# Moving elementwise work of a chunked linear attention from GpSimd to VectorE and ScalarE, and four more chunks from float16 parts

## The chip, the cores and the metric

The kernel runs on one core of one Trainium2 chip. The time is the device time of one execution in microseconds; the runs of the kernel before have a median of 1040.34 us (1038.24 to 1041.38, three runs). The engines are written as in the profile: PE is TensorE (PEld its weight loads), DVE is VectorE, ACT is ScalarE, POOL is GpSimd, SP is SyncE, which issues most of the DMAs.

## What is computed

Three layers follow one another, for 4 batches, 768 tokens and 384 features (8 heads of 48). The first is a linear attention whose state is multiplied by a complex decay at every token; the second and third are MLPs with a hidden size of 1536, each behind a mixing of the tokens.

```python
mag = sqrt(a_re**2 + a_im**2); scale = minimum(mag, 0.999) / (mag + 1e-6)
for t in range(S):                       # S = 768, state D x D = 48 x 48 per head
    S_re, S_im = ar*S_re - ai*S_im + outer(k[t], v[t]), ar*S_im + ai*S_re
    y[t] = q[t] @ S_re
x = y as (batch, token, 384)
u = x + (x^T @ U @ V)^T                  # low rank: U is 768 x 32, V is 32 x 768
x1 = u + relu(u @ w1) @ w2               # first MoE
u = x1 + real(fft2(x1)); un = normalised rows of u
out = u + relu(un @ w1') @ w2'           # second MoE
```

## The kernel before

**Attention.** The tokens of a batch are cut into 6 chunks of 128, and elementwise work is done for a pair of chunks at a time, on tiles of 128 partitions by 3 x 2 x 128 = 768 columns. Pairs are numbered m = 0 to 11; pairs 0 to 2 are batch 0. `decays(m)` takes logarithms and exponentials of the decays, scans their running product along the tokens (L340) and makes decayed queries and keys; `turns(m)` makes the angles, scans their running sum (L381), takes sine and cosine and writes the turned queries and keys as `QK`, one tile a chunk (L408, L409). Six DMAs a chunk, issued on SP, rearrange `QK` to `QT`, heads apart. `products(m, j)` then does one chunk: scores, masked scores, keys turned back by PE, output and next state. A chunk is "plain" where its products are plain float32; otherwise each operand is split into a float16 part and a float16 remainder, and three float16 products replace one. Before, the chunks of batch 0 and the first four of batch 1 are plain: `plain = b == 0 or b == 1 and c < 4`.

**MoE.** `moe_units` goes over batches, two halves of 384 tokens (g) and 12 blocks of hidden units (f). In a hidden step PE makes `hp` (nine matmuls), ACT its rectified high part `hh` (L182), DVE the low part `hl` (L184), and PE adds the step before to `acc` (nine matmuls of `hh`, `hl` and weights). High and low parts are float32 values cut to what PE multiplies exactly; L91, L92 and L93 are the three products of such pairs. `make_ut` makes the input of a half: transposed tokens plus the low-rank mixing, as high and low parts. `from_f64` unpacks weights that lie in DRAM as float64 words.

**Order.** The first MoE's loop for batch b weaves in the attention of batch b+1 at a fixed rate (`Side`, 58 or 48 steps over 40 slots), so that both share every engine; in batch 3's half g = 1 it weaves in the second MoE's weights and the DFT of batch 0. Each engine's instructions are put in an order before the run, by a planner that goes by priorities and its own costs; on the chip each engine takes its queue in that order, so an instruction that waits holds up all behind it. `hh` and `hl` are traced with high priority. Which engine takes an elementwise step is written out in place, as in

```python
E = G if b else V                                  # decays: L325 on POOL from pair 3 on
(G if m == 2 or b else V).tensor_tensor(th, s1_, th, ALU.mult)          # L349
(G if m in (1, 2) or b else V).tensor_tensor(s1_, s1_, s2_, ALU.mult)   # L354
(V if z else G).tensor_tensor(QK[:, z, :, 128:256], ...)                # L409
G.tensor_tensor(plo[:, hs], pm[hf], ph[:, hs], ALU.subtract)            # L446
```

The functions that the change touches stand here with the profile's line numbers; each float32 tile with the tag "t" takes one of six buffers that all pairs share.

Of the kernel before, what the change touches and what calls it, by code (L numbers as in the profile page):

```python
# [8 lines left out]
F16 = mybir.dt.float16  # L9
# [4 lines left out]
I16 = mybir.dt.int16  # L14
AF = mybir.ActivationFunctionType
# [6 lines left out]
DM = H * D  # L22
# [19 lines left out]
def mixer_kernel(ctx, tc, a_in, qk_in, v_in, u_in, v4_in, w_in, cc_in, ss_in, cb_in, sb_in, id_in, mask_in, rows_in, out):  # L42
# [69 lines left out]
    def from_f64(src, name, signs=False):  # L112
# [22 lines left out]
    def load_w(mi, f, z):  # L135
# [4 lines left out]
        x = from_f64(w_in[mi, f][:, zs], f"w{mi}_{f}_{z}", mi == 1 or f > 8)  # L140
# [50 lines left out]
    # ------------------------------------------------------------------ attention  # L191
# [27 lines left out]
    def load(kind, m):  # L219
        """Decays, or queries and keys, of a pair of chunks."""  # L220
# [11 lines left out]
    def load_vs():  # L232
        """All values of the first batch."""
# [18 lines left out]

    def parts(m):
        """The first pair goes chunk by chunk, so that its products start early."""
        return [slice(0, 1), slice(1, 2)] if m == 0 else [slice(0, 2)]

    def decays(m):
        """Decayed queries and keys of a pair of chunks and the tangents of its turns."""
# [3 lines left out]
        E = G if b else V  # L262

# [3 lines left out]
        if b == 0:  # L267
            T_, s1, s2 = a[:, 1], mk("L"), mk("s")
# [4 lines left out]
        Th = a[:, 0] if b == 0 else mk("Th")  # L273
# [3 lines left out]
        ew[m] = T_, Th, qf, kf, ends  # L277
# [947 lines left out]
```

## Time and profile before

| | |
|---|---|
| median of the runs | 1040.34 us |
| span of the profiled execution, first to last instruction | 1035.1 us (5.2 us under the median of the runs) |
| mean granted clock of TensorE | 0.949 |
| busy, share of the span | PE 86%, PEld 81%, DVE 67%, ACT 43%, POOL 43% |
| instructions | DVE 1104, ACT 841, POOL 426, PE 6338 |
| first hidden step of the first MoE | about 137.8 us |
| first hidden step of the second MoE | about 694.6 us |

Busy shares are means over stages with different limits. Where a share matters below, it is read for one stage. An engine's time is not lost by idling; what is lost is read from what ended the idle time. A span on POOL is rough, and the matmuls' ends are modelled.

### The profile page before, as it was taken

The numbers are of one execution on the slowest core, as the hardware profiler recorded it, in microseconds if no ns is written. First come the engines' busy times: TensorE is split into PE (matmuls) and PEld (weight loads), VectorE is DVE, ScalarE is ACT, GpSimd is POOL, SyncE is SP. The second block draws the span as 40 slices with busy tenths as digits, with TensorE's granted clock in tenths as the row PEclk, the third lists the DMA queues.
The fourth block names the chain that finished last, engine by engine and source line by source line (L and its number), as shares of the span: only waits on it lengthen the run. The fifth ranks groups of instructions, "written<-read, shape, count | busy, mean of one in ns | idle before, by whom it ended". The sixth has DMA issues, their size and how long they took to land. (4 is left out here: it accounts for less than half of the span.)

```text
span 1035.1 us, 16471 instructions
## 1 busy us (share of the span) xinstructions
PE 885.1 (86%) x6338; PEld 841.7 (81%) x6338; DVE 690.3 (67%) x1104; ACT 441.3 (43%) x841; POOL 443.3 (43%) x426
## 2 busy tenths in 40 slices
PE   0059978788778787798899999779999999999997
PEld 0048777578777787787899999779999999999997
DVE  7997988897877689788764727886535554362121
ACT  6436565657545555555643224465212211222111
POOL 4445646575464645656446307776312222020000
PEclk9999899979898898989899999889999999999999
DMA  8078646834516152614135103342101021000000
GB/s 346 0 103 165 194 81 138 166 69 109 94 45 121 49 93 69 115 48 93 33 61 200 39 1 115 108 144 77 62 16 47 2 77 46 1 23 19 7 23 27
DMA packets 47097, 83.43 MB, mean 81 GB/s; under 512 B 5600, under 2 KB 36064, under 8 KB 47008
## 3 DMA queue, kind: packets, MB, share of 16 engines
q1 hardware_dynamic: 45152, 75.96, 30.8%
q0 software_dynamic: 1856, 6.31, 1.7%
q8 instruction: 52, 0.85, 0.4%
q14 instruction: 37, 0.30, 0.1%
HBM read 53.79 MB, written 9.44 MB: 61 GB/s over the span
## 5 line engine op out<-in xcount | busy, mean ns | idle before, releaser
L184 DVE SCALAR_TENSOR_TENSOR hl<-hp,hh 128x384 fp32r<-128x384 f32 x192 | 105.4, 551 | 191.8 <-ACT hh L182 186.6
L182 ACT ACTIVATE hh<-hp 128x384 fp32r<-128x384 f32 x192 | 93.1, 488 | 270.9 <-PE hp L93 249.1
L91 PE MATMUL acc<-w,hh 128*128 128x384 f32 x576 | 202.4, 352 | 2.0 <-ACT hh L182 2.0
L93 PE MATMUL acc<-w,hl 128*128 128x384 f32 x576 | 166.1, 352 | 38.4 <-DVE hl L184 38.2
L92 PE MATMUL acc<-w,hh 128*128 128x384 f32 x576 | 197.4, 343 | 0.0
L93 PEld LDWEIGHTS acc<-w,hl 128*128 128x128 f32 x576 | 106.9, 195 | 45.4 <-DVE hl L184 45.1
L91 PEld LDWEIGHTS acc<-w,hh 128*128 128x128 f32 x576 | 111.4, 193 | 4.3 <-ACT hh L182 3.0
L92 PEld LDWEIGHTS acc<-w,hh 128*128 128x128 f32 x576 | 111.5, 194 | 0.0
L91 PE MATMUL hp<-u,w 128*128 128x384 f32 x288 | 103.0, 359 | 6.2 <-ACT w L141 3.1
L92 PE MATMUL hp<-u,w 128*128 128x384 f32 x288 | 103.7, 360 | 1.2 <-POOL u L630 1.0
L93 PE MATMUL hp<-u,w 128*128 128x384 f32 x288 | 102.4, 356 | 0.0
L92 PE MATMUL hp<-n,w 128*128 128x384 f32 x288 | 96.9, 336 | 1.6 <-DVE n L920 1.6
L91 PE MATMUL hp<-n,w 128*128 128x384 f32 x288 | 96.5, 336 | 1.1 <-ACT n L919 1.1
L93 PE MATMUL hp<-n,w 128*128 128x384 f32 x288 | 96.8, 336 | 0.0
L437 PE MATMUL sc<-QT 96*128 96x128 f32 x384 | 66.6, 328 | 11.4 <-DMA QT<-QK 10.5
L437 PEld LDWEIGHTS sc<-QT 96*128 96x128 f32 x384 | 60.7, 232 | 14.3 <-issue 11.3
L142 POOL TENSOR_TENSOR w<-wxw,w 128x384 fp32r<-128x384 f32 x48 | 58.8, 1235 | 21.9 <-ACT w L141 21.7
L451 PE MATMUL kp<-ident,QK 128*128 128x128 f32 x120 | 20.5, 297 | 53.7 <-POOL QK L409 48.6
L91 PEld LDWEIGHTS hp<-u,w 128*128 128x128 f32 x288 | 58.5, 203 | 7.0 <-ACT w L141 3.3
L451 PEld LDWEIGHTS kp<-ident,QK 128*128 128x128 f32 x120 | 16.1, 155 | 55.5 <-POOL QK L409 48.6
L92 PEld LDWEIGHTS hp<-u,w 128*128 128x128 f32 x288 | 58.6, 203 | 2.2 <-POOL u L630 1.6
L93 PEld LDWEIGHTS hp<-u,w 128*128 128x128 f32 x288 | 58.3, 203 | 0.0
(302 smaller groups left out, 2056.4 us busy)
## 6 DMA issues: line engine op xcount, KB each, us to landing
QT<-QK SPq DMA_DIRECT2D x144, 129.0 KB
stw<-in_w_dram SPq DMA_DIRECT2D x48, 384.0 KB
ain<-in_a_dram SPq DMA_DIRECT2D x12, 768.0 KB
qkin<-in_qk_dram SPq DMA_DIRECT2D x12, 768.0 KB
x1d<-x SPq DMA_DIRECT2D x24, 192.0 KB
vin<-in_v_dram SPq DMA_DIRECT2D x18, 192.0 KB
lo<-x1d SPq DMA_DIRECT2D x12, 192.0 KB
out_dram<-lo SPq DMA_DIRECT2D x12, 192.0 KB
```

The costliest lines, as they stand in the source:

```text
L91: T.matmul(o, ah, bh, start=start, stop=False, skip_group_check=skip)
L92: T.matmul(o, ah, bl, start=False, stop=False, skip_group_check=skip)
L93: T.matmul(o, al, bh, start=False, stop=stop, skip_group_check=skip)
L142: G.tensor_tensor(w[:, 1, zs], x, f32(w[:, 0, zs]), ALU.subtract)
L182: A.activation(hh, hp, AF.Relu)
L184: V.scalar_tensor_tensor(out=hl, in0=hp, scalar=0.0, in1=f32(hh), op0=ALU.max, op1=ALU.subtract)
L437: T.matmul(ps[:, h, :], q[:, 128:256], q[:, :128], start=True, stop=True)
L451: T.transpose(kp[z][:, i * 128 : (i + 1) * 128], QK[:, z, i, 128:256], ident)
```

## The change

Work moves between engines, and four chunks change their arithmetic. From pair 3 on, POOL keeps the tangent (L337) and the decayed key (L360) of a pair, the small `fe` of a chunk and the weights' low parts; DVE takes the products L349 and L354, both halves of the turned keys, the remainders `plo`, `S[2]` and `slo`, the scaling of the state (except in batch 0) and the low part of u. ACT takes the multiply-add of L325, the rounding multiply of L389, the two range checks in place of L291, and the in-place scaling of the keys in `QK` (L494) as three passes of a [P, 1] scale. The three scans of a pair become one over 768 columns, with uint8 multipliers that restart each row; queries and keys are turned by sine and cosine in one instruction of 768 columns each, for which both lie in one tile `turn`. The tag "t" goes from six buffers to four and `turn` takes the room of the other two. In `make_ut` the low-rank product is added in PSUM, on top of the transposes, so that the copy of `xs` and the addition on DVE go. Weights are given their sign by a bit operation on DVE, always. All of batch 1's chunks are made from float16 parts.

```diff
-        if signs:
-            A.activation(high.bitcast(F32), high.bitcast(F32), AF.Sign)
-            G.tensor_tensor(x, x, high.bitcast(F32), ALU.mult)
-        else:
-            V.scalar_tensor_tensor(out=xi, in0=high, scalar=-(2**31), in1=xi, op0=ALU.bitwise_and, op1=ALU.bitwise_or)
+        V.scalar_tensor_tensor(out=xi, in0=high, scalar=-(2**31), in1=xi, op0=ALU.bitwise_and, op1=ALU.bitwise_or)
...
-        def at(nm, tag=None, bufs=6, shape=(128, 3, 2, 128), dt=F32, pl=pl):
+        def at(nm, tag=None, bufs=4, shape=(128, 3, 2, 128), dt=F32, pl=pl):
...
-            T_, s1, s2 = mk("T"), mk("L"), mk("s")
+            turn = at(f"turn{b}_{cc[0]}", "turn", 1, (128, 2, 3, 2, 128))
+            T_, s1, s2 = turn[:, 1], mk("L"), mk("s")
...
-                steady(js)
+                if b == 0:
+                    steady(js)
+                else:
+                    A.activation(Th[:, :, js], re, AF.Relu, bias=least, scale=-1.0, accum_out=stat("im", b, cc[0]))
+                    A.activation(Th[:, :, js], s2_, AF.Relu, bias=most, accum_out=stat("im", b, cc[1]))
...
-            E.tensor_scalar(s2_, s2_, -2e-6, 1.0, ALU.mult, ALU.add)
+            A.activation(s2_, s2_, AF.Copy, bias=1.0, scale=-2e-6)
...
-            for i in range(3):
-                V.tensor_tensor_scan(out=row(s1, i, js), data0=starts[:, :n], data1=row(s1, i, js), initial=1.0, op0=ALU.max, op1=ALU.mult)
+            V.tensor_tensor_scan(out=flat(s1), data0=starts, data1=flat(s1), initial=1.0, op0=ALU.max, op1=ALU.mult)
...
-            (G if m == 2 or b else V).tensor_tensor(th, s1_, th, ALU.mult)
+            V.scalar_tensor_tensor(out=th, in0=s1_, scalar=FSCALE**2, in1=th, op0=ALU.mult, op1=ALU.mult)
...
-            (G if m in (1, 2) or b else V).tensor_tensor(s1_, s1_, s2_, ALU.mult)
+            V.scalar_tensor_tensor(out=s1_, in0=s1_, scalar=FSCALE**2, in1=s2_, op0=ALU.mult, op1=ALU.mult)
...
-            (G if m in (1, 2, 3, 4) else V).tensor_tensor(f, q, s1_, ALU.mult)
+            (G if m in (1, 2) else V).tensor_tensor(f, q, s1_, ALU.mult)
...
+            if len(jj) == 1:
+                if cy is not None:
+                    V.tensor_tensor(T_[:, :, 0, 0], T_[:, :, 0, 0], cy[:, :3], ALU.add)
+                V.tensor_tensor_scan(out=flat(Th), data0=going, data1=flat(T_), initial=0.0, op0=ALU.mult, op1=ALU.add)
...
-            V.tensor_scalar(t, th, 1.0 / (2 * PI), MAGIC, ALU.mult, ALU.add)
+            if b == 0:
+                V.tensor_scalar(t, th, 1.0 / (2 * PI), MAGIC, ALU.mult, ALU.add)
+            else:
+                A.activation(t, th, AF.Copy, bias=MAGIC, scale=1.0 / (2 * PI))
...
-                for z, w in ((1, T_), (0, Th)):
-                    V.tensor_tensor(QK[:, z, :, :128], qf[:, :, j], w[:, :, j], ALU.mult)
-                    (V if z else G).tensor_tensor(QK[:, z, :, 128:256], kf[:, :, j], w[:, :, j], ALU.mult)
+                w = turn[:, :, :, j]
+                for to, x in ((slice(128, 256), kf), (slice(0, 128), qf)):
+                    V.tensor_tensor(QK[:, :, :, to], x[:, :, j].unsqueeze(1).to_broadcast([128, 2, 3, 128]), w, ALU.mult)
+                for z in range(2):
                     for i in range(3):
                         p0 = z * 48 + i * 16
                         nc.sync.dma_start(QT[p0 : p0 + 16], QK[:, z, i, :])
...
-        plain = b == 0 or b == 1 and c < 4
+        plain = b == 0
...
-                G.tensor_tensor(plo[:, hs], pm[hf], ph[:, hs], ALU.subtract)
+                V.tensor_tensor(plo[:, hs], pm[hf], ph[:, hs], ALU.subtract)
...
-                for z in range(2):
-                    G.tensor_tensor(QK[:, z, :, 128:256], QK[:, z, :, 128:256], QK[:, z, :, 256:257].to_broadcast([128, 3, 128]), ALU.mult)
+                for i in range(3):
+                    A.activation(QK[:, :, i, 128:256], QK[:, :, i, 128:256], AF.Copy, scale=QK[:, 0, i, 256:257])
...
-                    G.tensor_tensor(sh, pS.rearrange("p (h e) -> p h e", h=8), f3, ALU.mult)
+                    V.tensor_tensor(sh, pS.rearrange("p (h e) -> p h e", h=8), f3, ALU.mult)
...
-            G.tensor_tensor(slo, sS, shi, ALU.subtract)
+            V.tensor_tensor(slo, sS, shi, ALU.subtract)
...
         def mix(k):
-            zv = bank(f"zv{b}_{g}_{k}")[:, :384]
-            T.matmul(zv, zst[b][:, k * 128 : (k + 1) * 128], vst[:, g * 384 : (g + 1) * 384], start=True, stop=True)
-            V.tensor_tensor(xs[k], zv, xs[k], ALU.add)
+            zv = bank(f"zv{b}_{g}_{k}")[:, :384] if first else xs[k]
+            T.matmul(
+                zv,
+                zst[b][:, k * 128 : (k + 1) * 128],
+                vst[:, g * 384 : (g + 1) * 384],
+                start=first,
+                stop=True,
+                skip_group_check=not first,
+            )
+            if first:
+                V.tensor_tensor(xs[k], zv, xs[k], ALU.add)
             u = pair(f"u{b}_{g}_{k}")
             A.copy(u[:, 0], xs[k])
-            (V if (b, g) == (0, 0) else G).tensor_tensor(u[:, 1], xs[k], f32(u[:, 0]), ALU.subtract)
+            V.tensor_tensor(u[:, 1], xs[k], f32(u[:, 0]), ALU.subtract)
```

Here `first` is true for batch 0's first half alone. `turn` of batch 0 is the tile of the decays, except for pair 2. The filling matmuls that run while PE has nothing to do keep their number and size, with other operands.

## Rows read from the trace of the kernel before

**Rows 1.** Stretches: us, busy time (instructions) of each engine, PE's granted clock, DMA.
```profile
0.00:137.80 137.80, 72.67 (x702) 59.32 (x703) 119.71 (x172) 73.28 (x131) 68.57 (x59) 0.96 0.59 152
137.80:315.80 178.00, 144.53 (x1134) 131.94 (x1132) 151.19 (x200) 104.79 (x188) 104.75 (x81) 0.90 0.51 107
315.80:463.80 148.00, 123.48 (x990) 116.89 (x989) 115.95 (x150) 83.21 (x152) 82.33 (x73) 0.89 0.38 75
463.80:583.80 120.00, 110.56 (x922) 107.39 (x922) 84.67 (x125) 57.06 (x112) 67.44 (x73) 0.96 0.38 92
...
627.70:694.60 66.90, 56.04 (x304) 52.85 (x304) 60.83 (x111) 32.28 (x69) 50.74 (x54) 0.91 0.39 121
```

**Rows 2.** Waits, total us, times, longest: 315.8 to 463.8, last row 137.8 to 315.8.
```profile
PE acc L93 <- DVE hl L184: 13.9, 6, 5.2
ACT s L87 <- DVE L L340: 13.4, 3, 7.6
DVE L L326 <- POOL s L325: 9.9, 2, 7.2
...
DVE L L326 <- POOL s L325: 6.3, 2, 5.4
```

**Rows 3.** Timeline of DVE and POOL (start, us, engine, line), around 36 and 131 us.
```profile
36.00 5.79 DVE L381 TENSOR_TENSOR_SCAN ain<-one,ain 128x128 f32<-128x128 f32 x3
37.72 1.91 POOL L360 TENSOR_TENSOR qkin<-qkin,s 128x768 f32<-128x768 f32 x1
...
44.39 0.94 DVE L313 SCALAR_TENSOR_TENSOR L<-s,L 128x768 f32<-128x768 f32 x1
...
45.67 1.22 DVE L381 TENSOR_TENSOR_SCAN ain<-one,cy,ain 128x128 f32<-128x128 f32 x3
...
131.82 1.49 DVE L627 TENSOR_TENSOR xs<-zv,xs 128x384 f32<-128x384 f32 x3 [0.53 <-PE zv L626]
...
136.04 1.85 DVE L381 TENSOR_TENSOR_SCAN Th<-one,T 128x256 f32<-128x256 f32 x3 [1.06 <-ACT T L87]
```

**Rows 4.** DVE's groups by form, whole run: busy us, mean ns, idle before.
```profile
L340 DVE TENSOR_TENSOR_SCAN L<-starts,L 128x256 f32<-128x256 bf16 x36 | 37.6, 1097 | 0.1
...
L381 DVE TENSOR_TENSOR_SCAN Th<-one,cy,T 128x256 f32<-128x256 f32 x18 | 29.5, 1683 | 0.0
...
L326 DVE SCALAR_TENSOR_TENSOR L<-L,s 128x768 f32<-128x768 f32 x12 | 26.3, 2189 | 17.0 <-POOL s L325 16.8
```

**Rows 5.** POOL's groups by form, 315.8 to 463.8 us.
```profile
L446 POOL TENSOR_TENSOR ph<-pm,ph 128x512 f16<-128x512 f32 x12 | 16.0, 1337 | 5.3 <-ACT ph L445 5.3
...
L409 POOL TENSOR_TENSOR QK<-s,Th 128x384 f32<-128x384 f32 x6 | 7.9, 1331 | 4.7 <-issue 2.7 <-ACT Th L87 2.0
L354 POOL TENSOR_TENSOR L<-L,s 128x768 f32<-128x768 f32 x3 | 7.9, 2648 | 1.8 <-DVE s L353 1.8
L630 POOL TENSOR_TENSOR u<-xs,u 128x384 fp32r<-128x384 f32 x6 | 7.6, 1270 | 4.4 <-ACT u L629 4.4
L568 POOL TENSOR_TENSOR Sl<-S,Sh 96x384 f16<-96x384 f32 x5 | 6.8, 1354 | 1.9 <-ACT Sh L567 1.9
L349 POOL TENSOR_TENSOR Th<-L,Th 128x768 f32<-128x768 f32 x3 | 5.5, 1828 | 10.2 <-ACT Th L348 10.2
```

**Rows 6.** ACT's groups by form, whole run: a pass of 768 columns.
```profile
L311 ACT ACTIVATE L<-ain 128x768 f32<-128x768 f32 x11 | 9.2, 833 | 3.9 <-DMA ain<-in_a_dram 3.9
```

**Rows 7.** Timeline of PE: state products of a plain and of a float16 chunk.
```profile
96.86 3.62 PE L469 MATMUL g<-vin,ke 128*64 128x48 f32 x32
...
381.50 0.36 PE L469 MATMUL g<-vh,kl 128*128 128x48 f16 x8
```

**Rows 8.** POOL's groups by form, whole run.
```profile
L128 POOL TENSOR_TENSOR wxw<-wxw,stw 128x384 f32<-128x384 f32 x30 | 32.3, 1078 | 24.1 <-DVE wxw L125 8.3 <-issue 6.3 <-ACT stw L127 2.9
...
L494 POOL TENSOR_TENSOR QK<-QK 128x384 f32<-128x384 f32 x22 | 19.9, 907 | 17.4 <-DMA QT<-QK 10.1 <-DVE hl L184 3.9 <-DVE kl L461 3.4
...
L491 POOL TENSOR_SCALAR fe<-QT 96x8 f32<-96x8 f32 x20 | 7.3, 366 | 41.4 <-DMA QT<-QK 30.5 <-DVE S L548 7.2 <-DVE hl L184 2.4
```

More of the change, by code (lines that the diff above doesn't have):

```diff
@@ L14 @@
 I16 = mybir.dt.int16
+U8 = mybir.dt.uint8
 AF = mybir.ActivationFunctionType
@@ L110, in kept, with from_f64 @@
             fn(*args, **kw)
-    def from_f64(src, name, signs=False):
+    def from_f64(src, name):
         n = src.shape[-1]
@@ L276, in decays @@
         jj = [slice(0, 2)]
-        ew[m] = T_, Th, qf, kf, ends
+        ew[m] = T_, Th, qf, kf, ends, a if b == 0 else turn
         def of(js, *xs):
@@ L288, in steady @@
         def steady(js):
-            re, s2_, th = of(js, a[:, 0], s2, Th)
+            re, s2_ = of(js, a[:, 0], s2)
             V.scalar_tensor_tensor(
-                out=th if b else unread(js), in0=s2_, scalar=RE_LEAST, in1=re, op0=ALU.add, op1=ALU.is_le, accum_out=stat("re", b, cc[js.start])
+                out=unread(js), in0=s2_, scalar=RE_LEAST, in1=re, op0=ALU.add, op1=ALU.is_le, accum_out=stat("re", b, cc[js.start])
             )
@@ L368, in turns @@
         at = attention_pool()
-        T_, Th, qf, kf, ends = ew[m]
+        T_, Th, qf, kf, ends, turn = ew[m]
         use(TRIG)
@@ L378, in turns @@
             t, th = T_[:, :, js], Th[:, :, js]
-            n = 128 * (js.stop - js.start)
-            for i in range(3):
-                V.tensor_tensor_scan(
-                    out=row(Th, i, js),
-                    data0=one.to_broadcast([128, n]),
-                    data1=row(T_, i, js),
-                    initial=0.0 if cy is None else cy[:, i : i + 1],
-                    op0=ALU.mult,
-                    op1=ALU.add,
-                )
-            V.tensor_scalar(t, th, 1.0 / (2 * PI), MAGIC, ALU.mult, ALU.add)
+            if len(jj) == 1:
+                if cy is not None:
+                    V.tensor_tensor(T_[:, :, 0, 0], T_[:, :, 0, 0], cy[:, :3], ALU.add)
+                V.tensor_tensor_scan(out=flat(Th), data0=going, data1=flat(T_), initial=0.0, op0=ALU.mult, op1=ALU.add)
+            else:
+                for i in range(3):
+                    V.tensor_tensor_scan(
+                        out=row(Th, i, js),
+                        data0=one.to_broadcast([128, 128]),
+                        data1=row(T_, i, js),
+                        initial=0.0 if cy is None else cy[:, i : i + 1],
+                        op0=ALU.mult,
+                        op1=ALU.add,
+                    )
+            if b == 0:
+                V.tensor_scalar(t, th, 1.0 / (2 * PI), MAGIC, ALU.mult, ALU.add)
+            else:
+                A.activation(t, th, AF.Copy, bias=MAGIC, scale=1.0 / (2 * PI))
             V.scalar_tensor_tensor(out=th, in0=t.bitcast(I16)[:, :, :, 0::2], scalar=-2 * PI, in1=th, op0=ALU.mult, op1=ALU.add)
@@ L492, in products @@
             if not plain:
-                for z in range(2):
-                    G.tensor_tensor(QK[:, z, :, 128:256], QK[:, z, :, 128:256], QK[:, z, :, 256:257].to_broadcast([128, 3, 128]), ALU.mult)
+                for i in range(3):
+                    A.activation(QK[:, :, i, 128:256], QK[:, :, i, 128:256], AF.Copy, scale=QK[:, 0, i, 256:257])
         yield
@@ L641, in make_ut @@
             return
-        turn(0)
-        yield
-        turn(1)
-        mix(0)
-        yield
-        turn(2)
-        yield
-        mix(1)
-        yield
-        mix(2)
-        yield
+        for k in range(3):
+            turn(k)
+            mix(k)
+            yield
+            if k < 2:
+                yield
     def extra1(b, g, t, acc):
@@ L949, in mixer_kernel @@
     attp = [apool.enter_context(tc.tile_pool(name="att", bufs=2)), None]
+    starts = attp[0].tile([128, 6, 128], U8, tag="starts", name="starts", bufs=1)
+    going = attp[0].tile([128, 3, 256], U8, tag="going", name="going", bufs=1)
+    for x, every, rest_ in ((starts, 1, 0), (going, 0, 1)):
+        G.memset(x, rest_)
+        G.memset(x[:, :, 0:1], every)
+    starts = starts.rearrange("p x t -> p (x t)")
+    going = going.rearrange("p i t -> p (i t)")
     first = ExitStack()
@@ L966, in mixer_kernel @@
             with tc.issue_after(after):
-                T.matmul(warm, starts[:, :128], starts, start=True, stop=True, skip_group_check=True)
+                T.matmul(warm, mask, wide.bitcast(F16), start=True, stop=True, skip_group_check=True)
     first.close()
```

52 lines of the change are left out of this document (33 added, 19 removed).

## Prediction

> **What bounds the kernel now.** I read the table of stretches first, cut where the hidden steps of each batch of the first MoE begin [rows 1]. The reader is to see two regimes ahead of 694.6 us. Up to 137.8 us the first batch's attention runs and DVE is busy 119.7 us. From there to 583.8 us the first MoE works on batches 0, 1 and 2 with the next batch's attention woven in; these stages take 178, 148 and 120 us. PE stands still for 33, 25 and 9 us of them and is granted 0.90, 0.89 and 0.96 of its clock; DVE is busy 151, 116 and 85 us. From 627.7 to 694.6 us, where the second MoE's weights are unpacked, DVE is busy 60.8 of 66.9 us. After that nothing which this change touches is left but the last weight pieces. So what the change is worth is decided before 694.6 us, mostly in DVE's queue.
>
> The waits of batch 1's stage say why [rows 2]: PE waits 13.9 us for `hl`, a short DVE instruction stuck behind long ones. DVE itself waits 9.9 us for one POOL instruction, L325 (6.3 us in batch 0's stage). ACT waits 13.4 us for DVE's scans, with the hidden step's `hh` queued behind.
>
> Then I asked why DVE is long. On the timeline three scans of 128 columns take 5.79 us while POOL runs one product after another, and the same three take 1.22 us ten microseconds later, when POOL is idle [rows 3]. The groups confirm it [rows 4]: scans of 256 columns average 1097 and 1683 ns, where three back to back take 1.85 us, 617 each; L326 averages 2189 ns, where another instruction of 768 columns takes 0.94 us [rows 3]. (1097-617)x36 + (1683-617)x18 + (2189-940)x12 = 17 + 19 + 15 = 51 us of DVE are lost in these three groups alone.
>
> The Trainium skill, "SBUF — State Buffer", section "Who interferes with whom", says that VectorE and GpSimd share a port pair as an exclusive lock: a VectorE instruction with two SBUF inputs and a GpSimd instruction that reads SBUF keep each other out for a whole instruction. The trace agrees: the scans of 5.79 us stand beside POOL products of 1.9 us each [rows 3]. By that rule nearly all overlap is lost time, which would give the first rival below; the rule also speaks against the change, since what moves to DVE has two SBUF inputs itself and can be kept out by what stays on POOL.
>
> **The price of a POOL microsecond.** How much DVE time comes back for each microsecond taken from POOL? From below: the three groups alone, 51 us, over the 374 busy us that POOL has in the five stretches of the table, 0.14. From above: all the time in which the two can coincide, and DVE is busy 78% of batch 1's stage (116 of 148), so 0.78. Other groups with two SBUF inputs (L291, L313, L353, L408, L409, L125) are left out of the lower bound, so it is too low; the MoE's own DVE instructions read PSUM, so the upper one is too high. I take 0.35.
>
> **The change, part by part.**
>
> *Taken from POOL.* In batch 1's stage the groups that go are L446, L409, L354, L630, L568 and L349, 16.0 + 7.9 + 7.9 + 7.6 + 6.8 + 5.5 us [rows 5], and ten of L494 at 0.91, 9 us [rows 8]: 61 of POOL's 82.3 us [rows 1]. At 0.35 DVE gets 21 us back. The other stages go by the same means: a pair of chunks frees 1.83 + 2.65 + 2x1.33 = 7.1, a float16 chunk 2x1.34 + 2x0.91 + 1.35 = 5.8, three mixing steps 3.8 us. The first batch's attention has one L349, two L354, six L409 (k with the cosine) and pair 3's decays: 19 us, 7 back. Batch 0's stage has four pairs, some three float16 chunks, six mixing steps and six sign products L128 of 1.08 [rows 8]: 28 + 17 + 8 + 6 = 59, 21 back. Batch 2's stage has two pairs, about four chunks and three steps: 41, 14 back. 627.7 to 694.6 has some 18 sign products: 19, 7 back.
>
> *Added to DVE.* Neighbouring DVE instructions overlap a little: three of 384 columns take 1.49 us in a row [rows 3], so I count 0.48 for 384 columns, 0.6 for 512 and 0.87 for 768. A pair from pair 3 on: L349 and L354 come (+1.74), the count of re (-0.87) and the rounding multiply (L389, about -0.5) go to ACT. Twice three scans become two long ones: the trace shows no scan of 768, so it lies between 1.85 us (three of 256 at no gain) and 0.87 (any instruction of 768); nearest is the first, and from (617-407)/128 = 1.6 ns a column, the 128s being 1.22/3 = 407, it comes to 1.45, so -0.8 for both. The carry add costs 0.2, and six products of 384 become four of 768, 2.9 to 3.5. Net +0.4 a pair. A float16 chunk: L446 twice, L556 and L568: 1.2 + 0.96 = +2.1. Low halves of u trade an add for a subtraction: 0. A sign product becomes one pass: +0.48. The four chunks of batch 1 that turn float16 add `vl`, two `kl` and `ql` (0.48 + 0.96 + 1.1), 2.5 each.
> Sums: first batch +1, with the copies of L325 going to ACT. Batch 0's stage: four chunks at 4.6, less 2 for the first, which has no state, +16; chunks 4 and 5, +3; six signs +3; four pairs +2: +24. Batch 1: 6x2.1 + 1 = +14. Batch 2: +11. 627.7 to 694.6: 18x0.48 = +9.
>
> *Added to ACT.* A pair: two more passes of 768 columns at 0.83 [rows 6] with an accumulator's read each, say 2x1.0, and the passes of L325 and L389 at 0.83: +3.7 us. A chunk: the in-place rescale as three passes of 256 columns, each between 0.28 (a third of 0.83) and 0.83; nearer the first: +1.2. ACT is busy 104.8 of 178 and 83.2 of 148 us [rows 1]; with four pairs, five rescales and float16 copies of about 13 us it comes to 139 of 178, with three pairs and six rescales to 101 of 148. Beside DVE's and PE's work that is covered as long as ACT does not wait; where it does, see the second rival.
>
> *PE.* The state products of a plain chunk take 3.62 us; of a float16 chunk eight take 0.36 from start to end, so 24 take at most 1.1 [rows 7]. Four chunks give 10 us or more. That lies in batch 0's stage, where DVE is the longer (151 against 145), so I count none; without that cover it is worth these 10. In `make_ut` the mixing product is the same matmul, now into the transposes' bank: 0 on PE, and on ACT a copy less.
>
> *Waits.* L325 moves behind its Exp on ACT, so L326 no longer waits for POOL: 9.9 and 6.3 us go [rows 2]; what is late next is ACT's copy, under 1 us a pair, so I credit 9 and 6. On four pairs of batch 0's stage two POOL products of 1.83 and 2.65 also become DVE ones of 0.87 in the chain to the turns, 11 us of latency; most of it hides under the MoE, I count 3. The QT transfers are the same six per chunk on SP, issued after the second product instead of after each: half a microsecond, counted 0.
>
> **The sum.** First batch -7 + 1 = -6. Batch 0's stage -21 + 24 - 6 - 3 = -6. Batch 1's -21 + 14 - 9 = -16. Batch 2's -14 + 11 = -3, and PE, busy 110.6 of 120 us, allows little more. 627.7 to 694.6: -7 + 9 = +2. Together -29 against the profiled span of 1035.1 us: 1006. The median of the runs shown is 1040.34 us, 5.2 over that span; with these around it **1011 us**.
>
> **The rivals.** About 0.3%, 3 us, is what a measurement of this kernel can tell from no change.
>
> *More comes back.* At 0.6, and with `hl` and the scans no longer late, PE sets the pace. The relief rises by 0.25x(19 + 59 + 61 + 19) = 40 us, batch 2 being capped: 971, and to 960 if PE's 10 us count too. For it: 5.79 against 1.22 us, and the waits of 13.9 and 13.4 us that hang on DVE alone [rows 2, 3]. Against: the moved work has the form that is kept out, with L360, L337 and the weights' low halves still on POOL.
>
> *ACT waits for transfers (slower).* The in-place rescale of k may not start before the QT transfers have read it. On POOL these transfers were waited for by `fe` (L491), 30.5 us over 20 chunks, and by the rescale after it, 10.1 us over 22 instructions, two a chunk [rows 8]: 1.5 + 0.9 = 2.4 us a chunk, with nothing urgent behind. On ACT `hh` stands behind it, and PE behind `hh`. 15 chunks at 2.4 us are 36 us, against the 29 gained: 1047, and up to 1060 where PE's clock falls with it. It decides from 2 us a chunk. Against: `hh` is put ahead with high priority, so the rescale will mostly come late.
>
> *DVE is filled (slower or same).* At 0.17 the five sums are -2, +5, -5, +4 and +6: +8, 1048 us; at 0.2 the sides cancel, 1037 to 1043. For it: DVE is already busy 85 and 91% in batch 0's stage and from 627.7 to 694.6 [rows 1], where the change adds most.
>
> **Chances.** Forecast 0.46, more comes back 0.25, ACT waits 0.12, DVE filled 0.07, cancelled 0.10. Faster 0.71, same 0.10, slower 0.19. The range runs from the upper end of the gain rival's half to the lower half of the slower ones, 974 to 1046; the forecast's own, at 0.28 to 0.45, is 995 to 1025.
>
> **What the changed profile would show.** Right: POOL under 25 us in batch 1's stage and DVE near 109, the mean of the instruction at L326 near 1 us, the waits for `hl` halved, batch 1's stage near 132 us and batch 0's near 172. Wrong: an ACT wait for QT<-QK above 2 us a chunk; batch 0's stage no shorter, with DVE at 160 us or more; 627.7 to 694.6 longer by over 5 us; or batch 0's stage under 155 us, which would say that the float16 chunks' PE time, counted as nothing, was on the path.

## The result, and the profile after

The changed kernel takes 1029.38 us (median of 10 runs, 1020.90 to 1037.73) against 1040.14 (10 runs, 1036.85 to 1042.35): ratio 0.9887, 95% interval 0.9859 to 0.9914. It is 10.8 us faster; forecast were 29. Its profiled execution spans 1027.8 us. I cut it where the hidden steps of each batch begin, as in [rows 1]; "best" is both_halves, one of four kernels of the experiments that take 994 to 996 us; its profiled execution spans 992.3. The ten runs of the changed kernel spread over 16.8 us, those of the kernel before over 5.5; the changed kernel's two longest ran at a granted clock of 0.925, its two shortest at 0.945 and 0.947, and no run tells what decides it.

| stage | before | forecast | after | best |
|---|---|---|---|---|
| first batch's attention | 137.8 | 131.8 | 144.1 | 133.7 |
| batch 0's | 178.0 | 172 | 177.4 | 173.4 |
| batch 1's | 148.0 | 132 | 134.3 | 126.1 |
| batch 2's | 120.0 | 117 | 123.7 | 111.6 |
| batch 3's, g = 0 | 43.9 | 43.9 | 43.4 | 43.4 |
| batch 3's, g = 1 | 66.9 | 69 | 62.0 | 62.1 |
| from the second MoE on | 340.5 | 340.5 | 342.9 | 342.0 |

The stretches of the changed kernel, columns as in [rows 1]:

```profile
0.00:144.10 144.10, 71.39 (x702) 57.41 (x703) 114.36 (x159) 78.79 (x143) 52.85 (x51) 0.88 0.59 146
144.10:321.50 177.40, 133.63 (x1009) 121.88 (x1008) 136.68 (x202) 129.57 (x234) 38.33 (x36) 0.84 0.52 103
321.50:455.80 134.30, 116.10 (x979) 110.03 (x978) 100.77 (x151) 96.88 (x178) 19.86 (x21) 0.94 0.47 89
455.80:579.50 123.70, 113.03 (x970) 107.98 (x970) 87.86 (x148) 65.08 (x125) 30.15 (x36) 0.94 0.39 87
622.90:684.90 62.00, 54.51 (x309) 50.29 (x308) 59.38 (x124) 25.91 (x54) 34.68 (x38) 0.97 0.43 129
```

Against [rows 1], DVE's busy time fell in these five from 532 to 499 us and POOL's from 374 to 176, but batch 0's stage kept its length. There DVE is 14.5 us less busy and PE 10.9, and PE stands still for 43.8 us instead of 33.5, at 0.84 of its clock instead of 0.90. So neither DVE's nor PE's work holds that stage, and I looked at the waits. Five of the whole run that the change bears on (us in total, times, longest):

```profile
ACT QK L509 <- DMA QT<-QK: 33.1, 28, 3.0
DVE S L571 <- POOL fe L506: 24.7, 6, 5.3
PE sc L452 <- DMA QT<-QK: 23.1, 6, 8.0
PE acc L94 <- DVE hl L181: 17.5, 14, 2.7
DVE QK L419 <- DMA QT<-QK: 10.3, 3, 4.0
```

L509 is the in-place rescale of the keys (L494 before), L571 the scaling of the state (L556), L452 the scores (L437), L506 `fe` (L491), L419 the first write into a new `QK` (L405). Four of the five wait for QT transfers, directly or through `fe`. The fifth, `hl`, is what the change was reckoned by, and it did fall, from 38.2 us in the whole run before, and in batch 1's stage from 13.9 [rows 2] to 3.0. One moment of the timeline of the changed kernel shows three of them at once, behind SP's transfers, on ACT, PE and DVE:

```profile
210.20 7.68 SPq L427 DMA_DIRECT2D QT<-QK  x12
...
216.86 0.51 ACT L509 ACTIVATE QK<-QK 128x256 f32<-128x256 f32 x1 [2.53 <-DMA QT<-QK]
...
219.13 2.85 PE L452 MATMUL sc<-QT 96*128 96x128 f32 x16 [3.09 <-DMA QT<-QK]
...
219.41 0.56 DVE L571 TENSOR_TENSOR S<-S,fe 96x384 f32<-96x384 f32 x1 [3.42 <-POOL fe L506]
```

Both chunks of a pair are sent in one block of twelve transfers, 0.64 us each on SP, and three engines stand behind it.

DVE's groups that answer to [rows 4] (busy us, mean ns, idle before):

```profile
L347 DVE TENSOR_TENSOR_SCAN L<-starts,L 128x768 f32<-128x768 uint8 x11 | 21.6, 1966 | 0.2
L389 DVE TENSOR_TENSOR_SCAN turn<-going,turn 128x768 f32<-128x768 uint8 x9 | 17.4, 1932 | 0.2 <-ACT turn L88 0.2
L334 DVE SCALAR_TENSOR_TENSOR L<-L,s 128x768 f32<-128x768 f32 x11 | 13.7, 1244 | 7.3 <-ACT s L333 7.3
```

### The profile page after: what moved, and what is told of

It is laid out like the page before. It is cut to its first block, busy times and chain, and to the rows that moved or that the text cites. A ratio compares the mean times of both kernels' runs of the same rounds, so it can differ in the third digit from the quotient of the medians.

```text
span 1027.8 us, 16147 instructions
## 1 busy us (share of the span) xinstructions
PE 866.9 (84%) x6250; PEld 820.4 (80%) x6250; DVE 665.8 (65%) x1142; ACT 480.9 (47%) x910; POOL 234.0 (23%) x257
## 4 chain that ended last, share of the span: by engine, by line
PE 53%; DVE 23%; DMA 10%; ACT 5%; issue 4%; SPq 4%; POOL 1%; DVEq 0%; POOLq 0%; ACTq 0%
DMA QT<-QK 7%; PE acc L94 7%; PE hp L93 7%; PE hp L94 7%; PE acc L92 7%; PE hp L92 7%; PE acc L93 6%; SPq L427 3%; PE sc L452 3%; DMA stw<-in_w_dram 2%; PE g L484 2%; PE y L484 2%; DVE f L839 1%; DVE QK L423 1%; DVE wxw L126 1%
## 5 line engine op out<-in xcount | busy, mean ns | idle before, releaser
L92 PE MATMUL acc<-w,hh 128*128 128x384 f32 x576 | 200.3, 348 | 8.0 <-ACT hh L179 7.9
L93 PE MATMUL acc<-w,hh 128*128 128x384 f32 x576 | 194.3, 338 | 0.0
L94 PE MATMUL acc<-w,hl 128*128 128x384 f32 x576 | 160.8, 349 | 17.8 <-DVE hl L181 17.5
L92 PEld LDWEIGHTS acc<-w,hh 128*128 128x128 f32 x576 | 108.9, 189 | 13.2 <-ACT hh L179 11.5
L93 PEld LDWEIGHTS acc<-w,hh 128*128 128x128 f32 x576 | 109.0, 190 | 0.5 <-POOL w L139 0.5
L92 PE MATMUL hp<-u,w 128*128 128x384 f32 x288 | 101.0, 355 | 6.5 <-ACT u L661 6.5
L93 PE MATMUL hp<-u,w 128*128 128x384 f32 x288 | 101.6, 353 | 1.6 <-DVE u L662 1.6
L94 PE MATMUL hp<-u,w 128*128 128x384 f32 x288 | 101.4, 352 | 0.3 <-POOL kl L523 0.3
L452 PE MATMUL sc<-QT 96*128 96x128 f32 x384 | 64.3, 328 | 31.5 <-DMA QT<-QK 23.1
L452 PEld LDWEIGHTS sc<-QT 96*128 96x128 f32 x384 | 59.6, 235 | 35.5 <-issue 31.5
L92 PEld LDWEIGHTS hp<-u,w 128*128 128x128 f32 x288 | 56.6, 198 | 7.7 <-ACT u L661 7.6
L93 PEld LDWEIGHTS hp<-u,w 128*128 128x128 f32 x288 | 57.2, 199 | 2.1 <-DVE u L662 2.1
L94 PEld LDWEIGHTS hp<-u,w 128*128 128x128 f32 x288 | 57.1, 198 | 0.6 <-POOL w L139 0.5
```

The lines of the kernel that those rows point to most:

```text
L92: T.matmul(o, ah, bh, start=start, stop=False, skip_group_check=skip)
L93: T.matmul(o, ah, bl, start=False, stop=False, skip_group_check=skip)
L94: T.matmul(o, al, bh, start=False, stop=stop, skip_group_check=skip)
L452: T.matmul(ps[:, h, :], q[:, 128:256], q[:, :128], start=True, stop=True)
```

## The experiments

Each kernel is timed in five rounds beside the kernel before, on one chip; ratios are to that. Their theories: the gain was lost **behind the QT transfers** (by the moves to ACT and DVE, and by products that finish late), or, the rival, it was **never there** because DVE got back too little.

**Two moves undone.** The rescale and the scaling of the state go back to POOL, together and each alone.

```diff
-                for i in range(3):
-                    A.activation(QK[:, :, i, 128:256], QK[:, :, i, 128:256], AF.Copy, scale=QK[:, 0, i, 256:257])
+                for z in range(2):
+                    G.tensor_tensor(QK[:, z, :, 128:256], QK[:, z, :, 128:256], QK[:, z, :, 256:257].to_broadcast([128, 3, 128]), ALU.mult)
...
-                    V.tensor_tensor(sh, pS.rearrange("p (h e) -> p h e", h=8), f3, ALU.mult)
+                    G.tensor_tensor(sh, pS.rearrange("p (h e) -> p h e", h=8), f3, ALU.mult)
```

both_pool: 

> The changed kernel with two moves undone: the in-place rescale of the keys and the scaling of the state are on POOL again (2 x 0.9 and 1.3 us a float16 chunk), so that ACT and DVE have no instruction behind the QT transfers there. Theory, that the waits of ACT (33 us for QT<-QK at the rescale) and of DVE (25 us for fe) took the expected gain: those rows vanish, batches 0 to 2's stages get 10 to 20 us shorter together, and the time is 1010 to 1020 us. Rival, that they lie beside other work: POOL's 45 us cost DVE 15 us at 0.35 and the time is 1030 to 1045 us.

1013.05 us, 0.9759 (0.9726 to 0.9793): 16 us faster than the changed kernel. The rival falls. The waits of both_pool:

```profile
ACT qh L515 <- DMA QT<-QK: 26.6, 6, 6.5
...
PE sc L452 <- DMA QT<-QK: 15.0, 4, 8.1
...
PE acc L94 <- DVE hl L181: 12.1, 10, 2.7
```

DVE's wait for `fe` is gone, but ACT still waits 26.6 us for the transfers, now at the next instruction that reads them (the cast of q). So ACT's 33 us of waiting at L509 were not what was saved.

rescale_pool: 

> The changed kernel with only the in-place rescale of the keys back on POOL. Both moves undone together gave 1013 us against 1029. Theory, that ACT's wait for the transfers (33 us over 15 chunks) with hh behind it is the larger part: 1015 to 1020 us, and DVE's wait for fe stays near 25 us. Rival, that DVE's wait for fe is the larger part: 1023 to 1030 us.

scale_pool: 

> The changed kernel with only the scaling of the state back on POOL. By the theory that ACT's wait is the larger part: 1021 to 1027 us, ACT's wait for QT<-QK stays near 33 us. By its rival, that DVE's wait for fe with hl and the masks behind it is the larger: 1014 to 1019 us.

1025.43 us, 0.9880 (0.9858 to 0.9902), and 1023.62 us, 0.9836 (0.9809 to 0.9864). By the ratios the first gives 1 us and the second 5, and both together 13 (16 by the medians). Neither is the larger part. That relieving one engine buys little while the other still stands behind the transfers is my reading; each ratio is uncertain by 2 to 3 us.

act_late (on the kernel both_halves, below): 

> The kernel of 995 us with the in-place rescale on ACT after all, but placed behind the first cast of the masked scores, when the transfers have long been read: the same 1.2 to 1.5 us of ACT a chunk without the wait for QT<-QK. If it was the wait that made the move dear, this costs little: 994 to 1002 us. If it was ACT's own time, or an ACT that is full: 1005 to 1015 us.

```diff
-                for z in range(2):
-                    G.tensor_tensor(QK[:, z, :, 128:256], QK[:, z, :, 128:256], QK[:, z, :, 256:257].to_broadcast([128, 3, 128]), ALU.mult)
...
         masked(0)
+        if not last and not plain:
+            for i in range(3):
+                with tc.issue_after(halved[0]):
+                    A.activation(QK[:, :, i, 128:256], QK[:, :, i, 128:256], AF.Copy, scale=QK[:, 0, i, 256:257])
```

`halved[0]` is the first cast of the masked scores. 1005.55 us, 0.9682 (0.9656 to 0.9708), against 994.60 with the rescale on POOL: 11 us lost with no wait for QT<-QK left at that line. So the move is dear without that wait too. Whether by ACT's 1.5 us a chunk or because the keys reach their transposes later there stays open (the transposes' weight loads wait only 1.7 us for them in all, which speaks for the first); a rescale on ACT into a tile of its own, which would tell, was not tried.

**The merged products.** Queries and keys are turned by halves again, all on DVE; first in the changed kernel (dma_halves), then with both moves undone (both_halves).

```diff
-                for to, x in ((slice(128, 256), kf), (slice(0, 128), qf)):
-                    V.tensor_tensor(QK[:, :, :, to], x[:, :, j].unsqueeze(1).to_broadcast([128, 2, 3, 128]), w, ALU.mult)
-                for z in range(2):
+                for z in (1, 0):
+                    for to, x in ((slice(0, 128), qf), (slice(128, 256), kf)):
+                        V.tensor_tensor(QK[:, z, :, to], x[:, :, j], w[:, z], ALU.mult)
                     for i in range(3):
                         p0 = z * 48 + i * 16
                         nc.sync.dma_start(QT[p0 : p0 + 16], QK[:, z, i, :])
```

dma_halves: 

> The changed kernel with queries and keys turned in four products of 384 columns, the sine's half first with its three transfers issued right behind it, as before the change; all four products stay on DVE. Theory, that the transfers leave too late in the changed kernel: DVE is 0.6 us a chunk longer, but PE's wait for QT<-QK at the scores falls from 23 us to about 12, and the time is 1020 to 1026 us. Rival, that the order of issue is worth nothing, as I counted it: the time is 1029 to 1040 us, with the row of 23 us as it is.

both_halves: 

> The changed kernel with the rescale and the scaling of the state on POOL and with queries and keys turned by halves, transfers issued behind each half. If the late transfers cost by these two waits alone, nothing is left for the order of issue to give: 1010 to 1016 us. If PE's own wait at the scores is on the path besides, the 8 us that the halves gave alone come on top: 1003 to 1009 us.

1021.14 us, 0.9820 (0.9796 to 0.9843), and 994.60 us, 0.9591 (0.9570 to 0.9611). The halves give 8 us beside the two waits, as expected, and 18 without them, ten more than expected. The row that was to fall did not, though (PE's wait at the scores: 21.1 us in dma_halves, 18.7 in both_halves against 15.0 in both_pool), so the cause had to be tried by itself. Stretches of both_halves:

```profile
0.00:133.70 133.70, 70.80 (x704) 56.72 (x704) 115.03 (x172) 78.88 (x143) 52.34 (x50) 0.96 0.61 158
133.70:307.10 173.40, 128.89 (x1002) 120.08 (x1003) 140.08 (x216) 119.39 (x212) 56.50 (x55) 0.86 0.54 106
307.10:433.20 126.10, 113.93 (x988) 108.88 (x987) 107.34 (x163) 91.23 (x164) 33.20 (x36) 0.97 0.45 95
433.20:544.80 111.60, 108.05 (x966) 103.83 (x965) 83.49 (x150) 60.06 (x116) 36.62 (x47) 0.98 0.44 98
```

halves_late (the loop of the transfers behind both halves in the text): 

> The kernel of 995 us (rescale and scaling of the state on POOL, queries and keys turned by halves) with one difference: the six transfers of a chunk are issued together behind its fourth product, not three behind each half. Theory, that the halves help because transfers leave earlier and overlap the products: it loses most of the 18 us again, 1007 to 1014 us. Rival, that shorter DVE instructions and the order they give are what helps: 994 to 1001 us.

dma_behind (the transfers' loop turned to `(0, 1)`): 

> The kernel of 995 us with the transfers' queue turned round: the half whose products are made last is issued first, so that all six transfers of a chunk wait for its fourth product. The products keep their order. Theory, that the halves help by letting transfers leave earlier: it falls back by more than half of the 18 us, 1004 to 1013 us, and the first transfer leaves about 4 us later than at 45.33 us. Rival, that the products' place in DVE's queue is what helps: 994 to 1000 us.

halves_swapped (both loops turned): 

> The kernel of 995 us with the other half first: products and transfers of the sine made by ACT's last pass come ahead of those made by its first. If the merged products of the changed kernel lose because their first one must wait for both passes (Abs and Sin, 1.1 us of 384 or 1.7 us of 768 columns), this loses the same: 1002 to 1013 us. If the order that follows from shorter instructions is what helps, it stays at 994 to 1000 us.

995.70, 994.07 and 995.29 us (0.9582, 0.9561, 0.9573). None moved what it was to move: each queue's order is made anew from when operands are ready, a transfer waits only for the products of its own half, and SP sends the first one at 45.35, 45.27 and 45.45 us, against 45.33. They are repeats of both_halves. The next two tie the order down, on the same kernel; `tc.issue_after(x)` keeps an instruction behind x in its queue, and `sent` and `made` are None at the start of each chunk:

```diff
                 for z in (0, 1):    # dma_forced: transfers, the late half first
                     for i in range(3):
                         p0 = z * 48 + i * 16
+                        with tc.issue_after(sent) if sent else ExitStack():
+                            sent = nc.sync.dma_start(QT[p0 : p0 + 16], QK[:, z, i, :]).ins
...
                 for z in (0, 1):    # products_forced: the late half first
                     for to, x in ((slice(0, 128), qf), (slice(128, 256), kf)):
+                        with tc.issue_after(made) if made else ExitStack():
+                            made = V.tensor_tensor(QK[:, z, :, to], x[:, :, j], w[:, z], ALU.mult).ins
```

dma_forced: 

> The kernel of 995 us with the transfers' queue turned round by force this time: the six transfers of a chunk keep the order in which the half made last goes first, so none leaves before the fourth product. The products stay free. Theory, that the halves help by early transfers: 1004 to 1013 us, first transfer at about 50 us instead of 45.33. Rival, that the products' place in the queue helps: 994 to 1000 us.

products_forced: 

> The kernel of 995 us with the four products of a chunk kept in a row behind both sine passes, as the merged ones are, and the transfers free. DVE then stands in nearly the order of the changed kernel around them, though the mixing at the end of the first batch stays undivided. If the wait for both passes (with the late transfers that follow from it) is what the merged products lose, this gives back what the first batch's end does not explain: 1002 to 1008 us. If the end of the first batch is most of the 18 us, 996 to 1001 us. If instead the form of the merged instruction is slow, it stays at 994 to 996 us.

dma_forced: 1013.21 us, 0.9754 (0.9724 to 0.9784): all 18 us gone, with products as free and as short as in both_halves. products_forced: 1021.06 us, 0.9823 (0.9792 to 0.9854), slower than any text gave it. SP's first rows (start, us) of both_halves, dma_forced, products_forced and the kernel before, in this order:

```profile
45.33 30.36 SPq L427 DMA_DIRECT2D QT<-QK  x24
```
```profile
50.22 31.71 SPq L430 DMA_DIRECT2D QT<-QK  x24
```
```profile
49.41 28.08 SPq L430 DMA_DIRECT2D QT<-QK  x24
```
```profile
51.03 27.42 SPq L412 DMA_DIRECT2D QT<-QK  x24
```

The changed kernel's first transfer leaves at 50.12 us. So holding back the transfers (by 4 to 5 us at the first chunk), with the products left free, costs as much as merging them. Two things stay open. Against the kernel before, the changed kernel's first transfer is not late but 0.9 us early: the merged products only kept it from leaving at 45 us. And the totals agree where the stages do not: at the end of batch 0's stage both_pool is 9.5 us behind both_halves and dma_forced 4.7, at the end of batch 2's 15.4 and 19.7. both_halves, too, sends whole pairs in blocks of twelve in batch 0's stage. Why products_forced loses 8 us more than the merged products is not known. The merged product itself is not slow: 0.95 to 1.00 us against two halves of 0.55 to 0.57.

**The price of a POOL microsecond.** On both_pool, the remainder `plo` goes back to POOL too.

three_pool: 

> The changed kernel with the rescale and the scaling of the state on POOL, and the remainder plo as well: 30 products of 128x512 of about 1.34 us, 40 us of POOL, for 30 x 0.6 = 18 us of DVE. This is the price of a POOL microsecond by itself, with nothing that waits for a transfer. At 0.35 DVE gets back 18 us and gives 14: 1009 to 1013 us. If the price is over 0.5, as DVE's shortened rows say, the products cost DVE more than they free, or make the remainder late for the output products: 1016 to 1025 us. Near 0.1, as the two instructions put back so far say, DVE gains 14 us net: 1000 to 1008 us.

1023.92 us, 0.9869 (0.9838 to 0.9901): 11 us slower. Batch 0's stage of both_pool, then of three_pool:

```profile
140.70:316.60 175.90, 136.75 (x1007) 127.04 (x1006) 135.62 (x198) 119.15 (x212) 53.12 (x54) 0.84 0.53 104
```
```profile
140.40:316.30 175.90, 133.07 (x1009) 123.74 (x1007) 139.61 (x186) 120.81 (x213) 72.82 (x67) 0.85 0.53 104
```

DVE has 12 instructions less and is 4.0 us busier. With 0.6 us for each, as I had counted, that is 11.2 us for 19.7 us of POOL, 0.57. By the same two columns the two moves undone cost almost nothing here: from the changed kernel to both_pool POOL gains 14.8 us in this stage and DVE, with 4 instructions less, is 1.1 us less busy.

One stage is not the kernel, though. Over the five stretches POOL gains 52.8 us from both_pool to three_pool, and DVE, without the 36 remainders, is only 1.9 us less busy: 19.7 us, 0.37. For the two moves undone it is 37.3 us of POOL and, with 12 scalings of 0.48 us less on DVE, 2.1 us more DVE: 0.21. Nor is batch 0's stage any longer in three_pool. Batch 1's stage of both_pool, then of three_pool, is:

```profile
316.60:445.90 129.30, 114.09 (x983) 109.46 (x982) 103.50 (x150) 91.22 (x163) 33.96 (x36) 0.95 0.48 93
```
```profile
316.30:458.20 141.90, 121.43 (x1027) 115.62 (x1026) 108.15 (x141) 93.11 (x167) 54.18 (x51) 0.90 0.43 80
```

It is 12.6 us longer, and batch 2's is 3.8 us shorter. Whether DVE's lost time makes that, or remainders that come late for PE, is not shown, so the 11 us by themselves are no price of POOL's time.

**The float16 part.** Alone on the kernel before (f16_alone), taken out of the changed kernel (plain_back), and taken out of both_halves (moves_only); `plain = b == 0` against `plain = b == 0 or b == 1 and c < 4`.

f16_alone: 

> The kernel before with one line of the change: batch 1's first four chunks from float16 parts too. Nothing moves off GpSimd. My theory, that DVE sets the pace of batch 0's stage in the kernel before: the PE time saved there (about 10 us) is hidden and the chunks bring 4 x 2.5 us to DVE and 4 x 5.8 us to POOL, so batch 0's stage is 5 to 20 us longer and the time is 1045 to 1060 us. Rival, that PE's time was on the path after all: batch 0's stage is 5 to 10 us shorter and the time is 1030 to 1035 us.

plain_back: 

> The changed kernel with that one line undone, so the move off GpSimd alone; batch 1's first four chunks are plain float32 again. If DVE sets the pace of batch 0's stage, DVE loses 4 x 4.6 us there and the time falls from 1029 to 1012 to 1022 us. If PE or the waits for transfers set it, PE's float32 products come back as 10 to 18 us and the time is 1035 to 1045 us. If four rescales on ACT that wait 2.2 us each were the loss of this stage, ACT's waits for QT<-QK fall from 33 us to about 20 and batch 0's stage gets shorter in spite of PE.

moves_only: 

> The kernel of 995 us with batch 1's first four chunks in plain float32 again: the float16 part by itself, once the waits for transfers are gone. In the kernel before the float16 part cost 21 us, in the changed kernel about nothing (1026.6 without, 1029 with). If POOL's work was what made it dear, it now gains, as PE's 10 us come back: without it 1000 to 1008 us. If DVE still sets batch 0's stage, it is still a loss or nothing: without it 985 to 996 us.

1059.60 us, 1.0198 (1.0175 to 1.0220); 1026.59 us, 0.9863 (0.9818 to 0.9909); 997.53 us, 0.9584 (0.9556 to 0.9613). On the kernel before the float16 part costs 21 us; in the other two it cannot be told from nothing. Batch 0's stage of moves_only shows the trade (both_halves' is above):

```profile
132.80:306.20 173.40, 144.69 (x1097) 129.50 (x1096) 127.79 (x197) 111.50 (x197) 44.59 (x36) 0.89 0.53 107
```

At equal length PE has 15.8 us more there, DVE 12.3 and ACT 7.9 less.

**The end of the first batch.** In the changed kernel the mixing at its end stands on DVE and ACT behind unpacked weights, one of which waits for its DMA; PE's last z ends at 126.8 us and the next matmul of the mixing comes 7 us later. Four weight pieces are moved behind the first hidden step, in the changed kernel (tail_clear) and in both_halves (tail_and_halves):

```diff
-                for _ in range((0, 2, 2, 2, 2, 2)[c]):
+                for _ in range((0, 2, 2, 2, 2, 0)[c]):
                     next(w1, None)
...
-        for _ in range(2):
-            next(w1, None)
...
     first_attention(w1)
+    for _ in range(4):
+        next(w1, None)
```

tail_clear: 

> The changed kernel with four of the weight pieces that are unpacked ahead of the first hidden step traced behind it instead, so that no weight instruction stands between the last z and u on DVE and ACT. Theory, that the 6 us which the first batch's stage lost were the mixing at its end, queued behind unpacking that waits for a DMA: the time from the last z to the first hidden product falls from 11.7 to about 5 us and with PE warm the stage from 144 to about 136 us: 1020 to 1024 us. Rival, that the stage is long because DVE waits for the transfers of QT earlier in it: it stays over 141 us, and 1026 to 1032 us.

tail_and_halves: 

> The kernel of 995 us with four weight pieces traced behind the first hidden step as well. Its order has the mixing at the end of the first batch undivided already, so the 9 us that this gave in the changed kernel should not come twice: 990 to 998 us. If the pieces delay the first batch in some other way, it gets to 985 to 988 us.

1020.31 us, 0.9813 (0.9778 to 0.9847), and 998.51 us, 0.9623 (0.9582 to 0.9665). PE's rows at the end of the first batch, of the kernel before, the changed kernel and tail_clear (`z` ends the attention, `hp` is the first hidden product):

```profile
128.05 0.91 PE L594 MATMUL z<-x,ust 128*128 128x384 f32 x2 [0.30 <-ACT x L559]
...
131.34 0.79 PE L626 MATMUL zv<-vst,zst 128*128 128x384 f32 x3 [1.94 <-DVE zst L605]
132.98 0.61 PE L91 MATMUL hp<-u,w 128*128 128x384 f32 x2 [0.84 <-ACT u L629]
```
```profile
125.18 1.65 PE L609 MATMUL z<-x,ust 128*128 128x384 f32 x2 [1.61 <-ACT x L574]
...
134.08 1.33 PE L650 MATMUL zv<-vst,zst 128*128 128x384 f32 x3 [6.41 <-DVE zst L620]
136.84 1.01 PE L92 MATMUL hp<-u,w 128*128 128x384 f32 x2 [1.43 <-ACT u L661]
```
```profile
130.97 1.65 PE L609 MATMUL z<-x,ust 128*128 128x384 f32 x2 [1.40 <-ACT x L574]
...
135.20 1.33 PE L650 MATMUL zv<-vst,zst 128*128 128x384 f32 x3 [1.73 <-DVE zst L620]
137.08 1.01 PE L92 MATMUL hp<-u,w 128*128 128x384 f32 x2 [0.55 <-ACT u L661]
```

From z to the first hidden product it is 6.1 instead of 11.7 us, but z itself comes 5.8 us later, and the stage ends at 142.4 instead of 144.1. So the theory holds for that wait and for the time, which is 9 us lower by the medians and 8 by the ratios, but not for the stage. These two traces cannot say what the wait costs: from 110 to 130 us PE is granted 0.50 of its clock in tail_clear and 0.78 and 0.73 in the changed kernel. Where the gain comes from is not settled. In tail_and_halves the first stage is 128.0 us and batch 0's 179.6: over the two stages nothing is gained on both_halves (307.6 against 307.1).

**The signs.** signs_pool: 

> The changed kernel with the signs of the weights made as before, by Sign on ACT and a product on POOL (all of the second MoE's, and the first's from block 9 on). The sum had this move at +2 us for the stretch in which the second MoE's weights are unpacked; the stretch came out 4.9 us shorter. If that was the signs' doing, the stretch goes from 62 back to 66 to 68 us and the time to 1033 to 1036 us. If it was something else (the copies and the part lost to POOL elsewhere), it stays at 61 to 63 us.

```diff
+            A.activation(high.bitcast(F32), high.bitcast(F32), AF.Sign)
+            G.tensor_tensor(x, x, high.bitcast(F32), ALU.mult)     # instead of the bit operation on DVE
```

1038.77 us, 0.9972 (0.9946 to 0.9997), 9 us slower than the changed kernel. Its profiled execution was one of its longest (1045.5 us), and its first batch alone is 10.6 us longer than the changed kernel's, so only the stretch in question is read from it:

```profile
633.40:703.50 70.10, 59.44 (x310) 54.70 (x309) 61.60 (x110) 32.98 (x71) 53.37 (x56) 0.89 0.40 119
```

70.1 against 62.0 us, with DVE 2 us busier in spite of 14 instructions less. The other traces agree: the stretch takes 61.8 to 62.7 us in all 17 kernels with the signs on DVE, and 66.9 to 70.1 in the three with them on ACT and POOL (the kernel before, f16_alone and this one). It was the signs.

## Why the prediction came out as it did

The direction and the place (batch 1's stage) were right; the time lay inside the range; the gain was 0.37 of the 29 us forecast. Two terms of the sum failed; a relief of DVE that was larger than counted hid part of it.

*What held.* Batch 1's stage came to 134.3 us (132 forecast), with POOL at 19.9, DVE at 100.8 and `hl` at 3.0 instead of 13.9 us. The instruction at L326 (now L334) fell from 2189 ns [rows 4] to 1244. ACT's 129.6 and 96.9 us are near the 139 and 101 counted.

*The price, if anything too low.* I took 0.35 of a microsecond of DVE for each of POOL. To estimate it afterwards I summed over DVE's instructions the time above the shortest one of the same line and form: 175 us before and 82 after in the five stretches. That is 94 us for the 198 that POOL lost, 0.47, if the whole fall is put down to POOL; the merged scans are in it too. three_pool, which moves POOL's work alone, gives 0.57 in one stage and 0.37 over the five. The work added to DVE, the shortest times summed, was 65 us against 59 counted. So DVE came out better than the sum said, 33 us less busy where it had 11 (-70 + 59), and the rival in which DVE is filled falls. The Trainium skill, "SBUF — State Buffer", section "Who interferes with whom", would have nearly all overlap lost between instructions of this form. The remainders of three_pool come near that in batch 0's stage (0.57, with DVE busy three quarters of the time); over the five stretches they (0.37) and the rescale and the state's scaling (0.21, and 0.06 in batch 0's stage) do not, and no run shows why.

*The step that failed* is "the QT transfers are the same six per chunk on SP, issued after the second product instead of after each: half a microsecond, counted 0". I counted the second product's length. But the merged product needs both sine passes, DVE's queue puts other work ahead meanwhile (on the first chunk a product of 768 columns and three scans), and no transfer can leave before the last product: the first left at 50.12 us, where with the halves it leaves at 45.33. With the two moves undone this term is worth 18 us, not 0 (both_halves against both_pool), and holding back the transfers alone costs as much (dma_forced). It is a gain missed rather than a delay, since the kernel before sent its first transfer at 51.03 us. By which waits the late transfers become 18 us stays open.

They do not explain why the first batch's stage grew from 137.8 to 144.1 us. The last z starts 2.9 us earlier than before; the first hidden product then comes 11.7 us after it instead of 4.9, and the first hidden step starts 7.3 us after that instead of 4.8. There PE stands still more and is granted less: from 120 to 140 us it is busy 5.9 and 2.9 us of each ten at 0.73 and 0.50 of its clock (0.50 is the lower level, 1.2 GHz), before 9.1 and 7.3 us at 1.00 and 0.83. Six kernels with merged products and the same first batch spend 140.4 to 152.4 us there, seven with halves 132.8 to 141.0; the 141.0 is dma_behind, whose first transfer leaves at 45.27 us and which is as fast as the others in all. So the first batch's lost gain was not traced to one cause; tail_clear, which moves the unpacking at its end, gives 8 to 9 us of the whole time back, but not in this stage.

*The second* is the cover given to ACT and DVE behind the transfers. "Covered as long as ACT does not wait" priced the rescale, and the rival met its threshold: 33.1 us over 15 chunks are 2.2 a chunk. Its mechanism is still not the one shown, since ACT waits 26.6 us in both_pool too, and 11 us stay lost in act_late where it does not wait at that line. The scaling of the state I counted as one more 0.48 us of DVE; I did not see that `fe`, which had been POOL's wait of 30.5 us [rows 8], then stands ahead of DVE's whole queue: 24.7 us of waits. Together the two moves cost 13 to 16 us; undoing one alone gave 1 or 5.

*Terms of other sizes.* The scan of 768 columns takes 1.75 us where nothing disturbs it, against 1.85 for three of 256 [rows 3], not the 1.45 estimated: 0.1 us gained, not 0.4. L325's wait, credited with 15 us, gave 9.5 (16.8 to 7.3 us, now for ACT's copy). The signs were +2 and came out at -5: I added DVE's pass and left out that POOL's product and ACT's Sign were links of the unpacking of each piece. ACT waited 8.8 us for that product in this stretch before, beside a POOL that was busy 50.7 of 66.9 us [rows 1]. Batch 2's +11 is +9 by its own terms (four chunks at 2.1, two pairs at 0.4). The float16 chunks were counted at +16 us of DVE in batch 0's stage and at nothing for PE. Taking them out (plain_back, moves_only) changes nothing that can be told, with PE 15.8 us busier and DVE 12.3 less: so the two cancel, and PE's time should have stood against DVE's.

Without the two failed steps the same change is worth 44.5 us (both_halves, 994.60 against 1039.14), more than the 29 forecast.

## What to carry to other kernels

Merging instructions that feed a DMA changes when the DMA can leave: count from the last operand of the merged one, then find what that queue puts ahead of it. An instruction that reads or overwrites what a DMA moves belongs on an engine with nothing urgent behind it, even a busy one (13 to 16 us here); and where several engines stand behind the same transfers, undo their waits together, since one alone shows little. In a planned kernel, read from the trace that an edit of the order has moved what it was to move.

## What the runs showed of the hardware

POOL's instructions were not alike to DVE in batch 0's stage: 19.7 us of remainders (128x512, float16 out) cost it 11 us, 14.8 us of in-place rescales and state scalings about 1. Over the five stretches the difference is smaller, 0.37 against 0.21 of a microsecond for each. A scan goes by its columns: 768 take 1.75 us in one instruction, 1.85 in three, where a product of 768 takes 0.95.
